# Long convolution with a gated projection on one Trainium2 core: first-stage loads of 16 spread rows, filter products of 128 rows by 200 columns, twiddles on GpSimd

## The chip, the core and the metric

The kernel runs on one core of a Trainium2 chip. A core has five engines that run their own instruction queues: TensorE (PE, matrix products into PSUM; its weight loads are shown apart as PEld), VectorE (DVE), ScalarE (ACT), GpSimd (POOL) and SyncE (SP, which here only issues transfers). Transfers between the device memory (DRAM) and the on-chip memory (SBUF, 128 partitions) run on 16 DMA engines; SP, ACT and POOL each issue transfers on queues of their own. The metric is the device time of one execution in microseconds (us), as a median of several runs.

## The reference

Inputs `x` and `v` are (4, 12800, 128). A small network makes a filter as long as the sequence; `u = x * v` is convolved with it along the sequence, gated by `x`, and then goes through a short causal convolution, a sigmoid gate and two projections.

```python
h_filt = (np.maximum(pos_emb @ w1, 0.0) @ w2) * np.exp(-0.01 * np.arange(S))[:, None]
y = irfft(rfft(x * v, 2 * S, axis=1) * rfft(h_filt, 2 * S, axis=0), 2 * S, axis=1)[:, :S]
x2 = x * y
gate = sigmoid(sum(conv_w[k] * shift(x2, KC - 1 - k) for k in range(KC)))
out = (gate * (x2 @ w_val)) @ w_out
```

## The kernel before

The sequence index is split as S = 12800 = J x N1 x N2 with J = 2 halves, N1 = 100 and N2 = 64. The long transform becomes one over n1 (100 values, index k1 after it), a twiddle, and one over n2 (64 values, k2 after it). Three stages follow each other:

1. First stage (pools `p1`, `ps1`; lines 237 to 394): the transform over n1 of `u`, written to the DRAM tensor `a_u`, and beside it the whole transform of the filter, which stays on the chip in `ag`.
2. Second stage (lines 397 to 527): for 50 pairs of k1, load `a_u`, transform over n2, multiply by the filter's spectrum, transform back, write to `c_y`.
3. Third stage (line 536 on): transform back over n1, multiply by `x`, short convolution, sigmoid, projections, output.

**First stage, the signal.** The host lays `x` and `v` out for each n2: two groups of two batches (h), each with 50 rows, because row n1 is folded with row 99 - n1 (index l). A group is filled up with 14 zero rows to 64, so that the two groups take partitions 0 to 63 and 64 to 127. One `fetch` (line 309) loads 128 rows of 8 KB into one of five tiles `held`; a sixth tile holds rows of `pos_emb`. The 64 values of n2 are taken in the order `n_seq`: q, 63 - q for q = 0 to 31. `product` (314) multiplies x by v on DVE. `mirrored` (320) makes sum and difference of the two of a pair q (tile `eo`, two buffers), and the difference over l. `spectra(q, s)` (329) multiplies with the table `fold`, 64 rows at a time, into PSUM `fp`, and ACT copies the result to `st`. `store` (343) writes rows 0 to 95 from ACT's queue and rows 96 to 99 from POOL's.

**First stage, the filter.** The generator `filt` (253) is worked off in pieces between the signal's steps: 16 parts of `pos_emb @ w1` (PE line 257, then DVE line 260 into `g_sb`, and the next load of `pos`); then the products over n1, with 4 columns e of the filter per piece (lines 275 and 276: one e, 64 columns wide, cosine and sine into the lower and upper 64 rows of `ap`; ACT copies them into `ag`, line 277); then 25 pieces of twiddles: ACT scales a 128 x 128 table by a column of `tw` (line 286), DVE adds the other scaled table (line 289, `fk`), PE multiplies `ag` by `fk` (line 297), ACT copies back (line 300).

**The order** is written out by hand (`tc.manual_schedule()`), so each engine runs its instructions in the order of the code. The main loop (line 368) has 64 steps n, two (s = 0, 1) for each q. In a step come: the fetch of n + 7, the product of n + 3, in even steps the sums of pair q + 1, the spectra of n, then pieces of the filter, then the store of n. Each piece yields a weight (1.5 for a part, 1.0 and 1.7 for products, 1.9 for twiddles); pieces are taken until their weights reach the share (n + 1) / 58 of the total of 115.2, so the filter is done by step 58. SP's queue has the fetches and the loads of `pos`; POOL's has the small stores, the early tables, and nothing else in this stage.

**Second stage, buffers.** `load_pair` takes tiles from the same pool `ld` (six tiles of 8 KB a partition): one table tile for each four pairs, one data tile a pair.

Of the kernel before, what the change touches and what calls it, by code (L numbers as in the profile page):

```python
# [23 lines left out]
B, S, D, FO, KC = 4, 12800, 128, 64, 5  # L24
J, N1, N2 = 2, 100, 64
M = N1 * N2
KG = 8
NF, NH = N1 // 2, 64
R = 4
WARM = 2  # L30
NC1 = N1 // 2 + 1
EDGE = J * N1 - 128


def _tables():
# [5 lines left out]
    off = 2 * np.pi * (np.outer(2 * n1[:NF] + 1, 4 * k1 + 1) % (8 * N1)) / (8 * N1)  # L41
    fold = np.zeros((128, 3, 128))
    for r in (0, NH):
        fold[r:r + NF, 0, :N1] = np.cos(off) + np.sin(off)
        fold[r:r + NF, 1, :N1] = np.cos(off) - np.sin(off)
    fold[:, 2] = 2 * fold[:, 0].astype(np.float32)


# [81 lines left out]
def tile_longconv_gate(  # L130
# [54 lines left out]
    xr_first = const.tile([D, R * B * N1], F32, name="xr_first")  # L185

    def load():
        return ld.tile([128, 2048], F32, name="ld")

    ag_pool = ctx.enter_context(tc.tile_pool(name="ag", bufs=1))  # L190
    ag = ag_pool.tile([128, N1, J, FO], F32, name="ag")
    ld_pool = tc.tile_pool(name="ld", bufs=6)
    ld = ld_pool.__enter__()


    CR = R * B * D
# [25 lines left out]
    def load_pair(p, n1=None):  # L222
        if p % PG == 0:
            n_p = min(PG, NP - p)
            wt = load().rearrange("p (k c e) -> p k c e", k=PG, c=4)[:, :, 0:3]
            nc.sync.dma_start(out=wt[:, 0:n_p], in_=t_w[:, p:p + n_p])
            weights.append(wt)
        a2 = load().rearrange("p (k j e) -> p k j e", k=2, j=J)
        if n1:
            load_a(a2, p, 0, n1)  # L230
        else:
            nc.sync.dma_start(
                out=a2.rearrange("p k j e -> p k (j e)"),
                in_=a_u[2 * p:2 * p + 2].rearrange("k s n e j b d -> (s n e) k (j b d)"))
        return a2, weights[-1][:, p % PG]

    with tc.tile_pool(name="p1", bufs=1) as p1, tc.tile_pool(name="ps1", bufs=1, space=PSUM) as ps1:
        g_sb = p1.tile([N1, J, FO, N2], F32, name="g_sb")

        GN, E, XB = 8, 4, 5  # L240
        held = [load() for _ in range(XB + 1)]
        PE1 = GN // 2 * N1
        pos_held = held.pop()[:, 0:2048 // PE1 * PE1].rearrange("p (i q a) -> p i q a", q=GN // 2, a=N1)
        parts, pos_ts = [(c0, j) for c0 in range(0, N2, GN) for j in range(J)], []

        def load_pos():
            if len(pos_ts) < len(parts):
                c0, j = parts[len(pos_ts)]
                t = pos_held[:, len(pos_ts) % (2048 // PE1)]
                nc.sync.dma_start(out=t.rearrange("p q a -> p (q a)"), in_=pos[j, c0 // GN])  # L250
                pos_ts.append(t)

        def filt():
            for i, (n0, j) in enumerate(parts):
                gp = ps1.tile([N1, GN, FO], F32, name="gp", bufs=2)
                for q in range(GN // 2):
                    nc.tensor.matmul(
                        out=gp[:, 2 * q:2 * q + 2].rearrange("a n e -> a (n e)"),
                        lhsT=pos_ts[i][:, q], rhs=w1bd, start=True, stop=True)
                nc.vector.scalar_tensor_tensor(  # L260
                    g_sb[:, j, :, n0:n0 + GN], gp.rearrange("a n e -> a e n"), 0.0,
                    win[:, j, n0:n0 + GN].unsqueeze(1).to_broadcast([N1, FO, GN]),
                    op0=ALU.max, op1=ALU.mult)
                load_pos()
                yield 1.5

            for j in range(J):
                for e0 in range(0, FO, E):
                    ap = ps1.tile([128, E, N1], F32, name="ap", bufs=2)
                    for e in range(E):  # L270
                        terms = [(j, 0, 1)] if j == 0 else [(1, 0, 1), (0, 1, 2)]
                        for i, (jj, wr, wi) in enumerate(terms):
                            lhs = g_sb[:, jj, e0 + e]
                            fl = dict(start=(i == 0), stop=(i == len(terms) - 1))
                            nc.tensor.matmul(out=ap[0:N2, e], lhsT=lhs, rhs=fwd[:, wr], **fl)
                            nc.tensor.matmul(out=ap[N2:2 * N2, e], lhsT=lhs, rhs=fwd[:, wi], **fl)
                    nc.scalar.copy(
                        out=ag[:, :, j, e0:e0 + E].rearrange("p k e -> p e k"), in_=ap)
                    yield 1.0 + 0.7 * j

            after = None
            for k0 in range(0, N1, 4):
                fk = p1.tile([128, 4, 2 * N2], F32, name="fk", bufs=2)
                for i in range(4):
                    k1 = k0 + i
                    nc.scalar.activation(fk[:, i], dft[:, 1], AF.Copy, scale=tw[:, 1, k1:k1 + 1])
                for i in range(4):
                    k1 = k0 + i
                    nc.vector.scalar_tensor_tensor(
                        fk[:, i], dft[:, 0], tw[:, 0, k1:k1 + 1], fk[:, i], op0=ALU.mult, op1=ALU.add)  # L290
                if after:
                    after()

                def after(k0=k0, fk=fk):
                    gz = ps1.tile([128, 4, 2 * N2], F32, name="gp", bufs=2)
                    for i in range(4):
                        nc.tensor.matmul(
                            out=gz[:, i], lhsT=ag[:, k0 + i].rearrange("p j e -> p (j e)"), rhs=fk[:, i],
                            start=True, stop=True)
                    nc.scalar.copy(out=ag[:, k0:k0 + 4].rearrange("p k j e -> p k (j e)"), in_=gz)  # L300
                yield 1.9
            after()
            yield 0.5

        XE = B * D // 2

        n_seq = [n for q in range(N2 // 2) for n in (q, N2 - 1 - q)]

        def fetch(i):
            t = held[i % XB]  # L310
            nc.sync.dma_start(out=t, in_=xv[n_seq[i]].rearrange("h q w j l b d -> (h q) (w j l b d)"))
            fetched[i] = t.rearrange("p (w e) -> p w e", w=2)

        def product(i):
            t = fetched.pop(i)
            u = p1.tile([128, J * 2 * XE], F32, name="u", bufs=1) if i % 2 == 0 else t[:, 0]
            nc.vector.tensor_tensor(u, t[:, 0], t[:, 1], op=ALU.mult)
            us[i] = u

        def mirrored(q):  # L320

            a, b = us.pop(2 * q), us.pop(2 * q + 1)
            eo = held_e[q % 2]
            for s, op in ((0, ALU.add), (1, ALU.subtract)):
                nc.vector.tensor_tensor(eo[:, s].rearrange("p j l e -> p (j l e)"), a, b, op=op)  # L325
                nc.vector.tensor_tensor(eo[:, s, :, 0], eo[:, s, :, 0], eo[:, s, :, 1], op=ALU.subtract)
            eos[q] = eo

# [20 lines left out]
        fetched, us, eos = {}, {}, {}  # L349
        with tc.manual_schedule():  # L350
            held_e = [p1.tile([128, 2, J, 2, XE], F32, name=f"eo{i}") for i in range(2)]
            fetch(0)
            raws = [
                (dst, _raw(p1, tables, src, f"raw{i}"))
                for i, (dst, src) in enumerate(((wval, w_val), (wout, w_out), (cw, conv_w.rearrange("k d -> d k"))))]
            fil = filt()
            narrow = (None for dst, raw in raws for _ in _narrow(nc, p1, dst, raw))
            n_fil, spent = 16 * 1.5 + 16 * 1.0 + 16 * 1.7 + 25 * 1.9 + 0.5, 0.0
            for i in range(1, XB):
                fetch(i)  # L360
                load_pos()
            product(0)
            product(1)
            mirrored(0)
            product(2)
            for i in (XB, XB + 1):
                fetch(i)
            for n in range(N2):
                q, s = divmod(n, 2)
                if n + XB + 2 < N2:  # L370
                    fetch(n + XB + 2)
                if n + 3 < N2:
                    product(n + 3)
                if s == 0 and q + 1 < N2 // 2:
                    mirrored(q + 1)
                st = spectra(q, s)
                while spent < n_fil * (n + 1) / (N2 - 6):
                    step = next(fil, None)
# [18 lines left out]
    with tc.tile_pool(name="p2", bufs=1) as p2, tc.tile_pool(name="psz", bufs=1, space=PSUM) as psz, \  # L397
# [62 lines left out]
        with tc.manual_schedule():  # L460
            for p in range(-1, NP + 1):
# [52 lines left out]
                    v_p[p] = va, vc, vd  # L514
                if nxt:
                    spectrum(p + 1, 1)
                if old:
# [259 lines left out]
```

## Time and profile before

| | |
|---|---|
| median of three runs | 1134.86 us (1127.76 to 1135.0) |
| profiled execution | 1130.9 us, of it the profiled span 1128.9 us |
| mean granted TensorE clock | 0.972 |
| busy share of the span | PE 92%, PEld 43%, DVE 87%, ACT 55%, POOL 62% |
| data moved | HBM read 225.76 MB, written 131.07 MB |
| of it by queue, share of the 16 DMA engines' span | SP's 224.74 MB, 55.0%; ACT's 129.18 MB, 29.3%; POOL's 2.94 MB, 0.9% |

The page has one execution, in parts: busy time by engine; the span in 40 slices of 28.2 us with a digit for the busy tenths; the DMA queues; the chain of work that ended last, followed backwards; the costliest groups of instructions, named by line of the kernel, engine, operation, output and inputs; and the transfers. In rows of groups, `x64` is a count; then come busy time and mean ns of one, then the engine's idle time before them and who ended it. In rows of the timeline the first number is the start in us, the second the duration. The store of POOL in step n (line 345) is a handy mark of the step. In the chain, `DMA ld<-in_xv_dram`, the loads of x and v, has 17% of the span; the three largest PE lines of the second stage together have 31%.

### The profile page before, as it was taken

The page shows a single profiled execution, that of the slowest core. Times are in us where ns is not written, and L with a number is a line of the kernel's source. Part 1 is how long each engine was busy: PE and PEld are TensorE (multiplying, and loading weights), DVE is VectorE, ACT ScalarE, POOL GpSimd, SP SyncE. Part 2 cuts the span into 40 slices and gives each one's busy share as a digit, 9 for nine tenths or more (in the row PEclk, how much of TensorE's full clock was granted, in tenths as well). Part 3 has the DMA queues.
Part 4 walks back from the last instruction along what each step waited for, and adds up shares of the span by engine and source line. Part 5 has one row for each costly group of instructions (what it writes and reads, how often), then busy time and mean ns, then how long its engine had stood idle before and what let it go on. Part 6 is the DMA issues. An engine that isn't in the chain of part 4 may idle for free.

```text
span 1128.9 us, 17155 instructions
## 1 busy us (share of the span) xinstructions
PE 1038.0 (92%) x6204; PEld 490.9 (43%) x6204; DVE 980.8 (87%) x1214; ACT 619.1 (55%) x1003; POOL 698.1 (62%) x405
## 2 busy tenths in 40 slices
PE   5789997977868999999999999979999999999996
PEld 2345654534423444444444444434444444444442
DVE  6677657888817999999999999739999999999997
ACT  1347665866642444444344444346767777767673
POOL 1111110100016888898898889638999899999981
PEclk9899999999986999999999999998999999999999
DMA  9999999999987788888988999566888888888842
GB/s 376 414 415 410 395 380 368 391 371 372 338 263 245 257 302 310 304 298 309 315 302 288 373 339 329 163 193 262 342 318 346 305 349 314 350 313 351 314 181 116
DMA packets 87771, 357.95 MB, mean 317 GB/s; under 512 B 9269, under 2 KB 18278, under 8 KB 65073
## 3 DMA queue, kind: packets, MB, share of 16 engines
q1 hardware_dynamic: 45768, 224.74, 55.0%
q10 hardware_dynamic: 39408, 129.18, 29.3%
q0 software_dynamic: 2512, 2.94, 0.9%
q8 instruction: 50, 0.82, 0.3%
q14 instruction: 33, 0.26, 0.1%
HBM read 225.76 MB, written 131.07 MB: 316 GB/s over the span
## 4 chain that ended last, share of the span: by engine, by line
PE 63%; DMA 22%; DVE 11%; ACT 3%; issue 1%; SPq 0%; ACTq 0%; DVEq 0%
PE c_ps L442 20%; DMA ld<-in_xv_dram 17%; PE sd L601 9%; PE z_ps L426 9%; PE o_ps L664 7%; PE v_ps L654 6%; PE tp L615 5%; PE fp L338 3%; DMA ld<-in_pos_dram 3%; PE c_ps L411 2%; DVE gt L643 2%; DVE eo L325 2%; DMA c_y<-c_sb 1%; DVE va L432 1%; DVE vb L432 1%
## 5 line engine op out<-in xcount | busy, mean ns | idle before, releaser
L628 POOL TENSOR_TENSOR ext<-yr,xr 128x400 f32<-128x400 f32 x120 | 304.4, 2538 | 38.1 <-DVE yr L626 32.7
L643 DVE SCALAR_TENSOR_TENSOR gt<-ext,cw,gt 128x1600 f32<-128x1600 f32 x128 | 242.7, 1896 | 2.4 <-ACT gt L640 2.4
L338 PE MATMUL fp<-eo,fold 64*128 64x512 f32 x768 | 194.8, 643 | 35.2 <-ACT st L340 19.0
L446 ACT COPY c_sb<-c_ps 128x1024 f32<-128x1024 f32 x100 | 101.3, 1013 | 207.3 <-PE c_ps L442 207.3
L345 POOL DMA_DIRECT2D a_u<-st x64 | 33.2, 519 | 290.4 <-ACT st L340 245.2
L340 ACT COPY st<-fp 128x1024 f32<-128x1024 f32 x128 | 126.7, 1016 | 117.9 <-PE fp L338 81.7
L442 PE MATMUL c_ps<-va,ld 64*128 64x512 f32 (+1 forms) x800 | 165.7, 554 | 0.0
L432 DVE TENSOR_TENSOR va<-z_ps,h_sb 128x2048 f32<-128x2048 f32 x50 | 114.5, 2290 | 30.4 <-PE z_ps L426 30.4
L426 PE MATMUL z_ps<-ld 64*64 64x512 f32 x800 | 123.0, 619 | 9.8 <-DMA ld<-a_u 8.7
L601 PE MATMUL sd<-ag,fold 100*64 100x512 f32 (+1 forms) x512 | 127.9, 617 | 2.9 <-DMA ag<-c_y 2.9
L509 POOL TENSOR_TENSOR va<-va,vb 128x1024 f32<-128x1024 f32 x49 | 116.0, 2367 | 15.9 <-DVE vb L432 15.9
L338 PEld LDWEIGHTS fp<-eo,fold 64*128 64x128 f32 x768 | 73.4, 199 | 115.4 <-issue 59.8
L442 PEld LDWEIGHTS c_ps<-va,ld 64*128 64x128 f32 x800 | 74.1, 189 | 112.2 <-issue 111.7
L664 PE MATMUL o_ps<-gd,wout 128*128 128x400 f32 x256 | 111.5, 517 | 10.7 <-DVE gd L659 9.8
L513 POOL TENSOR_TENSOR va<-va,vb 128x1024 f32<-128x1024 f32 x50 | 119.1, 2383 | 0.0
L432 DVE TENSOR_TENSOR vb<-z_ps,h_sb 128x2048 f32<-128x2048 f32 x50 | 114.0, 2281 | 0.0
L608 ACT COPY sd_sb<-sd 128x512 f32<-128x512 f32 x128 | 76.7, 599 | 57.6 <-PE sd L601 57.0
L654 PE MATMUL v_ps<-ext,wval 128*128 128x400 f32 x256 | 107.3, 501 | 0.0
L442 PE MATMUL c_ps<-vc,ld 64*128 64x512 f32 x400 | 94.2, 589 | 0.0
L615 PEld LDWEIGHTS tp<-ident,sd_sb 128*128 128x128 f32 x512 | 58.9, 142 | 79.2 <-PE sd L601 48.7
L510 POOL TENSOR_TENSOR vc<-vc,vd 128x768 f32<-128x768 f32 x49 | 89.2, 1820 | 1.9
L615 PE MATMUL tp<-ident,sd_sb 128*128 128x128 f32 x512 | 81.0, 283 | 4.7 <-ACT sd_sb L608 3.4
(86 smaller groups left out, 1484.9 us busy)
## 6 DMA issues: line engine op xcount, KB each, us to landing
ld<-in_xv_dram SPq DMA_DIRECT2D x64, 1024.0 KB
ag<-c_y SPq DMA_DIRECT2D x58, 1024.0 KB
c_y<-c_sb ACTq DMA_DIRECT2D x100, 512.0 KB
a_u<-st ACTq DMA_DIRECT2D x64, 768.0 KB
ld<-a_u SPq DMA_DIRECT2D x48, 1024.0 KB
xr<-in_xt_dram SPq DMA_DIRECT2D x31, 800.0 KB
out_dram<-o_sb ACTq DMA_DIRECT2D x31, 800.0 KB
ld<-in_tab_w_dram SPq DMA_DIRECT2D x12, 768.0 KB
```

The lines of the kernel that those rows point to most:

```text
L338: nc.tensor.matmul(out=fp[:, h], lhsT=fold[r, w], rhs=eo[r, o, :, l], start=i == 0, stop=i == len(terms) - 1)
L340: nc.scalar.copy(out=st[:, o].rearrange("k j (h b) d -> k h j (b d)", h=2), in_=fp)
L426: nc.tensor.matmul(out=zs[c][half[h]], lhsT=wk[half[c], 0, half[h]], rhs=a2[half[c], h, j], start=True, stop=True)
L432: nc.vector.tensor_tensor(out, z.rearrange("p (b d) -> p b d", d=D).unsqueeze(1).to_broadcast([128, n, B, D]), h_sb.unsqueeze(2).to_broadc ...
L442: nc.tensor.matmul(out=c_ps[:, h, 0:n], lhsT=wk[half[h], 1 + c], rhs=vt[half[h]].rearrange("p b d -> p (b d)"), start=(i == 0), stop=(i == ...
L513: nc.gpsimd.tensor_tensor(va[:, 2:4], va[:, 2:4], vb[:, 2:4], op=ALU.add)
L601: nc.tensor.matmul(out=sd[c * N2:(c + 1) * N2], lhsT=inv[k, s // NG, c], rhs=ct[c][k, r * B * D:(r + 1) * B * D], start=True, stop=True)
L615: nc.tensor.transpose(out=tp[:, b], in_=t[:, b], identity=ident)
L628: nc.gpsimd.tensor_tensor(e[:, r0 + r], yr, xr, op=ALU.mult)
L643: nc.vector.scalar_tensor_tensor(gt, rows(t, k), cw[:, k:k + 1], gt, op0=ALU.mult, op1=ALU.add)
L654: nc.tensor.matmul(out=v_ps, lhsT=wval, rhs=rows(t)[:, r * ROW:(r + 1) * ROW], start=True, stop=True)
L664: nc.tensor.matmul(out=o_ps, lhsT=wout, rhs=gd, start=True, stop=True)
```

## The change

The change is in the first stage and in how tiles of `ld` are handed out.

*Loads.* The host now lays out one block for each pair q, with both of its n2 (index e) in a row of 16 KB. The 50 rows of a group are spread over its 64 partitions: 48 of them on the partitions whose number modulo 8 is 0 to 5, two more on 6 and 38 (`QROW`); the table `fold` is spread in the same way. A fetch loads partitions r, r + 8, ..., r + 120 with one transfer, for r = 0 to 5 from SP's queue, and the four rows at 6, 38, 70 and 102 with one from POOL's. Zero rows are no longer loaded, except with q = 0, which has all eight r; the tiles of q = 1 and 2 are cleared once by DVE and POOL. There are three tiles of two slots each in place of five of one.

*The order.* In an odd step come the product of pair q + 2 (two instructions) and the fetch of q + 5, which writes the tile that this product has read; the sums stay in even steps. `pos` is loaded in four transfers into the still empty `ag`.

*The filter.* A product over n1 takes two e as 128 columns of weights and both halves of the table as 200 columns; ACT's copy of one piece falls into four, of 64 partitions and 200 columns each. The scaling of the twiddle tables moves from ACT to POOL. The weights become 0.33, 1.0 and 0.9, with a total of 60.3.

*Second stage.* Slots of `ld` come from a list `spare`; a data slot goes back after its pair's second `spectrum`, a table slot after the last use of its four pairs.

```diff
+KX = 6
+QROW = np.array([8 * (q // 6) + q % 6 if q < 48 else 6 + 32 * (q - 48) for q in range(NF)])
...
-        fold[r:r + NF, 0, :N1] = np.cos(off) + np.sin(off)
+        fold[r + QROW, 0, :N1] = np.cos(off) + np.sin(off)
...
     def load():
-        return ld.tile([128, 2048], F32, name="ld")
+        return ld[:, spare.pop(0)]
...
+    ld = ld_pool.__enter__().tile([128, 6, 2048], F32, name="ld")
+    spare, used = [4, 5, 0, 1, 2, 3], {}
...
+        def load_pos(i):
+            nc.sync.dma_start(out=pos_ts[:, 4 * i:4 * i + 4].rearrange("p i q a -> p (i q a)"), in_=pos[i])
...
-                yield 1.5
+                yield 0.33
...
-                    ap = ps1.tile([128, E, N1], F32, name="ap", bufs=2)
...
+                    ap = ps1.tile([128, E // 2, 2, N1], F32, name="ap", bufs=2)
+                    for e in range(E // 2):
+                        terms = [(j, 0)] if j == 0 else [(1, 0), (0, 1)]
+                        for i, (jj, w) in enumerate(terms):
+                            nc.tensor.matmul(
+                                out=ap[:, e].rearrange("p c k -> p (c k)"),
+                                lhsT=g_sb[:, jj, e0 + 2 * e:e0 + 2 * e + 2].rearrange("p e n -> p (e n)"),
+                                rhs=fwd[:, w:w + 2].rearrange("p c k -> p (c k)"),
+                                start=(i == 0), stop=(i == len(terms) - 1))
+                    for h in range(2):
+                        for c in range(2):
+                            nc.scalar.copy(
+                                out=ag[c * N2:(c + 1) * N2, :, j, e0 + h:e0 + E:2].rearrange("p k e -> p e k"),
+                                in_=ap[h * N2:(h + 1) * N2, :, c])
+                    yield 1.0
...
-                    nc.scalar.activation(fk[:, i], dft[:, 1], AF.Copy, scale=tw[:, 1, k1:k1 + 1])
+                    nc.gpsimd.tensor_scalar_mul(fk[:, i], dft[:, 1], tw[:, 1, k1:k1 + 1])
...
-                yield 1.9
+                yield 0.9
...
+        def fetch(q):
+            t = ld[:, 2 * (q % XB):2 * (q % XB) + 2].rearrange("p e n -> p (e n)")
+            for r in range(KX if q else 8):
+                nc.sync.dma_start(out=t[r:128:8], in_=xv[q, r])
+            if q:
+                nc.gpsimd.dma_start(out=t[KX:128:32], in_=xv[q, KX, 0:16:4])
+            fetched[q] = t.rearrange("p (e w n) -> p e w n", e=2, w=2)
+
+        def product(q):
+            t = fetched.pop(q)
+            us[q] = p1.tile([128, 2, J * 2 * XE], F32, name="u", bufs=1)
+            for e in range(2):
+                nc.vector.tensor_tensor(us[q][:, e], t[:, e, 0], t[:, e, 1], op=ALU.mult)
...
+            for q in range(1, XB):
+                (nc.vector, nc.gpsimd)[q - 1].memset(ld[:, 2 * q:2 * q + 2], 0.0)
             fetch(0)
+            load_pos(0)
...
+            product(0)
+            mirrored(0)
+            for q in range(1, XB):
+                fetch(q)
+                load_pos(q)
+            load_pos(XB)
             product(1)
...
                 if s == 0 and q + 1 < N2 // 2:
                     mirrored(q + 1)
+                if s == 1 and q + 2 < N2 // 2:
+                    product(q + 2)
+                    if q + 2 + XB < N2 // 2:
+                        fetch(q + 2 + XB)
                 st = spectra(q, s)
```

More of the change, by code (lines that the diff above doesn't have):

```diff
@@ L43, in _tables @@
     for r in (0, NH):
-        fold[r:r + NF, 0, :N1] = np.cos(off) + np.sin(off)
-        fold[r:r + NF, 1, :N1] = np.cos(off) - np.sin(off)
+        fold[r + QROW, 0, :N1] = np.cos(off) + np.sin(off)
+        fold[r + QROW, 1, :N1] = np.cos(off) - np.sin(off)
     fold[:, 2] = 2 * fold[:, 0].astype(np.float32)
@@ L187, in load @@
     def load():
-        return ld.tile([128, 2048], F32, name="ld")
+        return ld[:, spare.pop(0)]
     ag_pool = ctx.enter_context(tc.tile_pool(name="ag", bufs=1))
     ag = ag_pool.tile([128, N1, J, FO], F32, name="ag")
-    ld_pool = tc.tile_pool(name="ld", bufs=6)
-    ld = ld_pool.__enter__()
+    ld_pool = tc.tile_pool(name="ld", bufs=1)
+    ld = ld_pool.__enter__().tile([128, 6, 2048], F32, name="ld")
+    spare, used = [4, 5, 0, 1, 2, 3], {}
     CR = R * B * D
@@ L224, in load_pair @@
             n_p = min(PG, NP - p)
+            used["w", p // PG] = spare[0]
             wt = load().rearrange("p (k c e) -> p k c e", k=PG, c=4)[:, :, 0:3]
@@ L227, in load_pair @@
             weights.append(wt)
+        used["a", p] = spare[0]
         a2 = load().rearrange("p (k j e) -> p k j e", k=2, j=J)
@@ L238, in tile_longconv_gate @@
         g_sb = p1.tile([N1, J, FO, N2], F32, name="g_sb")
-        GN, E, XB = 8, 4, 5
-        held = [load() for _ in range(XB + 1)]
+        GN, E, XB = 8, 4, 3
         PE1 = GN // 2 * N1
[L243 to L251, printed above, removed]
+        parts = [(c0, j) for c0 in range(0, N2, GN) for j in range(J)]
+        pos_ts = ag.rearrange("p k j e -> p (k j e)")[:, 0:len(parts) * PE1].rearrange(
+            "p (i q a) -> p i q a", q=GN // 2, a=N1)
+        def load_pos(i):
+            nc.sync.dma_start(out=pos_ts[:, 4 * i:4 * i + 4].rearrange("p i q a -> p (i q a)"), in_=pos[i])
         def filt():
@@ L258, in filt @@
                         out=gp[:, 2 * q:2 * q + 2].rearrange("a n e -> a (n e)"),
-                        lhsT=pos_ts[i][:, q], rhs=w1bd, start=True, stop=True)
+                        lhsT=pos_ts[:, i, q], rhs=w1bd, start=True, stop=True)
                 nc.vector.scalar_tensor_tensor(
@@ L263, in filt @@
                     op0=ALU.max, op1=ALU.mult)
-                load_pos()
-                yield 1.5
+                yield 0.33
             for j in range(J):
                 for e0 in range(0, FO, E):
-                    ap = ps1.tile([128, E, N1], F32, name="ap", bufs=2)
[L270 to L279, printed above, removed]
+                    ap = ps1.tile([128, E // 2, 2, N1], F32, name="ap", bufs=2)
[13 more added lines that the diff above has]
+                    yield 1.0
             after = None
@@ L305, in tile_longconv_gate @@
         XE = B * D // 2
[L307 to L318, printed above, removed]
+        def fetch(q):
[10 more added lines that the diff above has]
+                nc.vector.tensor_tensor(us[q][:, e], t[:, e, 0], t[:, e, 1], op=ALU.mult)
         def mirrored(q):
-            a, b = us.pop(2 * q), us.pop(2 * q + 1)
+            u = us.pop(q)
             eo = held_e[q % 2]
             for s, op in ((0, ALU.add), (1, ALU.subtract)):
-                nc.vector.tensor_tensor(eo[:, s].rearrange("p j l e -> p (j l e)"), a, b, op=op)
+                nc.vector.tensor_tensor(eo[:, s].rearrange("p j l e -> p (j l e)"), u[:, 0], u[:, 1], op=op)
                 nc.vector.tensor_tensor(eo[:, s, :, 0], eo[:, s, :, 0], eo[:, s, :, 1], op=ALU.subtract)
@@ L357, in tile_longconv_gate @@
             narrow = (None for dst, raw in raws for _ in _narrow(nc, p1, dst, raw))
[L358 to L361, printed above, removed]
+            n_fil, spent = 16 * 0.33 + 32 * 1.0 + 25 * 0.9 + 0.5, 0.0
             product(0)
+            mirrored(0)
[3 more added lines that the diff above has]
+            load_pos(XB)
             product(1)
[L364 to L367, printed above, removed]
+            fetch(XB)
+            fetch(XB + 1)
             for n in range(N2):
                 q, s = divmod(n, 2)
[L370 to L373, printed above, removed]
                 if s == 0 and q + 1 < N2 // 2:
                     mirrored(q + 1)
+                if s == 1 and q + 2 < N2 // 2:
+                    product(q + 2)
+                    if q + 2 + XB < N2 // 2:
+                        fetch(q + 2 + XB)
                 st = spectra(q, s)
@@ L516, in tile_longconv_gate @@
                     spectrum(p + 1, 1)
+                    spare.append(used.pop(("a", p + 1)))
                 if old:
@@ L525, in tile_longconv_gate @@
                     inverse(p - 1, 1, ((0, oa[:, 2]), (1, oa[:, 3, 0:PB]), (0, oc[:, 0]), (1, oc[:, 1])))
+                    if p % PG == 0:
+                        spare.append(used.pop(("w", p // PG - 1)))
     ld_pool.__exit__(None, None, None)
@@ L756 @@
     xv = np.stack(pairs, 3)
-    xv = np.concatenate([xv, np.zeros_like(xv[:, :, :NH - NF])], 2)
+    xz = np.zeros(xv.shape[:2] + (NH,) + xv.shape[3:], xv.dtype)
+    xz[:, :, QROW] = xv
+    xz = np.stack([xz[:N2 // 2], xz[:N2 // 2 - 1:-1]], 1).reshape(N2 // 2, 2, 16, 8, -1)
+    xv = np.transpose(xz, (0, 3, 2, 1, 4)).reshape(N2 // 2, 8, 16, -1)
     pos = np.asarray(inputs["pos_emb"]).reshape(J, N1, N2 // KG, KG // 2, 2, FO)
-    pos = np.transpose(pos, (0, 2, 4, 5, 3, 1)).reshape(J, N2 // KG, 2 * FO, KG // 2 * N1)
+    pos = np.transpose(pos, (2, 0, 4, 5, 3, 1)).reshape(4, 4, 2 * FO, KG // 2 * N1)
+    pos = np.transpose(pos, (0, 2, 1, 3)).reshape(4, 2 * FO, 2 * KG * N1)
     feeds[:0] = [("xv", xv), ("xt", xt), ("pos", pos)]
```

## The prediction

> **What bounds the kernel now.** I read the page's slices first, then the table of windows, then the DMA queues. In the slices the first stage is the first eleven or twelve of 40.
>
> ```profile
> PE   5789997977868999999999999979999999999996
> DVE  6677657888817999999999999739999999999997
> DMA  9999999999987788888988999566888888888842
> ```
>
> Windows (length, then busy us of PE, PEld, DVE, ACT, POOL, then granted clock, DMA share, GB/s) of the n1 products, of the twiddles, and of the second stage:
>
> ```profile
> 113.00:141.00 28.00, 28.00 (x318) 17.07 (x318) 19.24 (x27) 19.22 (x21) 3.12 (x6) 1.00 1.01 396
> 226.00:254.00 28.00, 20.77 (x100) 11.19 (x98) 22.82 (x41) 17.60 (x35) 2.60 (x5) 0.94 0.99 370
> 400.00:700.00 300.00, 300.00 (x2204) 132.60 (x2204) 296.28 (x278) 124.38 (x196) 269.63 (x159) 1.00 0.90 314
> ```
>
> The second stage is PE's, 300 of 300 us. In the first the DMA engines are full (0.99 to 1.01), but others stand close behind: PE 28 of 28 in the n1 products, DVE 22.8 of 28 in the twiddles.
>
> Next, the DMA queues over 14 to 310 us (q1 carries SP's loads, q10 ACT's stores, q0 POOL's: packets, MB, share of 16 engines), what the products of line 317 waited for (us, times), and four of the 64 small stores of POOL, one for each step n. The first shown is the 6th (n = 5), the last the 64th (n = 63).
>
> ```profile
> q1 hardware_dynamic: 11192, 66.82, 58.7%
> q10 hardware_dynamic: 6384, 44.83, 37.9%
> q0 software_dynamic: 2210, 2.65, 2.9%
>   DMA ld<-in_xv_dram: 47.6, 19
> 49.15 0.52 POOL L345 DMA_DIRECT2D a_u<-st  x1 [8.93 <-ACT st L340]
> ...
> 141.58 0.52 POOL L345 DMA_DIRECT2D a_u<-st  x1 [3.72 <-ACT st L340]
> 145.94 0.52 POOL L345 DMA_DIRECT2D a_u<-st  x1 [3.84 <-ACT st L340]
> ...
> 331.56 0.52 POOL L345 DMA_DIRECT2D a_u<-st  x1 [2.58 <-ACT st L340]
> ```
>
> From n = 5 to n = 63 are 58 steps in 282.4 us, 4.87 each; by the shares loads take 2.86 of it, stores 1.85, the rest 0.15. Where the loads had been fetched ahead a step took 4.36 (141.58 to 145.94). DVE waits 47.6 us for loads in all: more than that no load can give back.
>
> **The change part by part.** *Fewer bytes.* Loads fall from 64 x 1024 KB = 67.1 MB to 2048 + 31 x 1600 KB = 52.9 MB. q1 moves 66.82 / (0.587 x 296) = 0.385 MB per us of all 16 engines, so 14.2 MB less are 37 us. At that rate loads take 2.86 x 52.9/67.1 = 2.25 us a step and DMA 4.25.
>
> *Fewer partitions per load.* One load of 1024 KB over 128 partitions becomes loads of 256 KB into 16 partitions (and 64 KB into 4). The second stage's end has narrow loads of `ag`: 512 KB into partitions 0 to 63, 128 KB into 16 neighbours. First their issue rows; then q1 in 606:608.5 (the first wide one, alone) and in 728:732 (16 neighbours only); then q1 and q10 in 727.5:729.5.
>
> ```profile
> ag<-c_y SPq DMA_DIRECT2D x4, 512.0 KB
> ag<-c_y SPq DMA_DIRECT2D x10, 128.0 KB
> q1 hardware_dynamic: 53, 0.43, 76.6%
> q1 hardware_dynamic: 114, 0.48, 89.0%
> q1 hardware_dynamic: 65, 0.33, 93.4%
> q10 hardware_dynamic: 125, 0.22, 31.0%
> ```
>
> Per us of 16 engines that is 0.43 / (0.766 x 2.5) = 0.225 MB into 64 partitions, 1.71 times slower than 0.385, and 0.48 / (0.89 x 4) = 0.135 MB into 16 neighbours, 2.85 times slower. Which partitions a load writes sets its price. Every eighth partition of 128 has no row here. The ends are 1.0 (spread as wide as a full load) and 2.85 (as few rows as the narrow one); nearest is 1.71, wide but not full. Two things soften it. A load is held up by other loads only, and these hold 0.587 of the time: 1 + 0.71 x 0.587 = 1.42, so loads 3.19 and DMA 5.2 a step. And a store runs beside a load that is held: in the last two rows the queues add up to 124%. I give back a tenth: **4.7 a step**. The ends are 4.25 and, at 1.71 with no softening, 5.85 (2.85 would make 8.4 by the same sum; the range leaves this out). So most of the 37 us are spent again.
>
> [...]
>
> *Issues.* Instead of one issue a step, SP has three and POOL half a one; a POOL issue is 0.52 (rows above) and POOL is busy 2.6 of 28 us, so the cost is cover only, but the order matters (next part). The loads into tiles 1 and 2 wait for a memset of 4096 columns; fetch 0 and the first filter rows, 2.9 MB or 7.5 us of DMA, go first and cover it. The larger filter loads and the earlier filter rows fall into the first five steps, where DMA is full either way; I leave n = 5 at 49 us.
>
> *The n1 products.* Columns here: busy us, mean ns of one, idle before.
>
> ```profile
> L275 PE MATMUL ap<-fwd,g_sb 100*64 100x100 f32 x384 | 37.5, 252 | 0.0
> L297 PE MATMUL gp<-fk,ag 128*128 128x128 f32 x200 | 32.1, 307 | 16.4 <-DVE fk L289 16.4
> L277 ACT COPY ag<-ap 128x400 f32<-128x400 f32 x32 | 26.4, 885 | 7.9 <-PE ap L276 7.9
> L340 ACT COPY st<-fp 128x1024 f32<-128x1024 f32 x128 | 126.7, 1016 | 117.9 <-PE fp L338 81.7
> ```
>
> 384 pairs of 100 columns (line 275 beside line 276) keep PE 37.5 us, 0.98 ns a column; 192 instructions of 200 columns are the same 38,400 columns, and at line 297's 32.1 / (200 x 128) = 1.25 ns a column 48 us at most. PE gains nothing; a step of 4.36 stays one. On ACT one copy of 885 ns becomes four of 200 columns each: 0.44 to 0.885, I take 0.5. The products cost 1.0 each of a budget of 60.3 over 58 steps, 1.04 a step: ACT 126.7/64 + 4 x 0.5 x 1.04 = 4.1 a step (end 5.7). Both lie under 4.7.
>
> *Twiddles on GpSimd.* In that part DVE works in this order (start, us):
>
> ```profile
> 235.50 1.23 DVE L317 TENSOR_TENSOR ld<-ld 128x1024 f32<-128x1024 f32 x1 [2.91 <-DMA ld<-in_xv_dram]
> ...
> 236.82 1.23 DVE L325 TENSOR_TENSOR eo<-u,ld 128x1024 f32<-128x1024 f32 x1
> ...
> 240.56 1.13 DVE L289 SCALAR_TENSOR_TENSOR fk<-dft,tw,fk 128x128 f32<-128x128 f32 x4
> ...
> 241.61 1.22 DVE L317 TENSOR_TENSOR u<-ld 128x1024 f32<-128x1024 f32 x1
> ```
>
> Two steps hold two products of 1.26, 3.74 of sums (236.82 to 240.56), and fk groups of 1.1, now 2 x 1.04/0.9 = 2.31 of them: 8.8 us, 4.4 a step. All these read two SBUF operands. What POOL does beside such an operation the third stage shows: durations (min/median/max ns), then one meeting.
>
> ```profile
> L628 POOL TENSOR_TENSOR ext<-yr,xr x120: 1026/2610/2645, 754.3 to 1102.4; 128x400 f32<-128x400 f32 x120
> L643 DVE SCALAR_TENSOR_TENSOR gt<-ext,cw,gt x128: 1868/1886/2119, 757.5 to 1116.2; 128x1600 f32<-128x1600 f32 x128
> 900.80 1.87 DVE L643 SCALAR_TENSOR_TENSOR gt<-ext,cw,gt 128x1600 f32<-128x1600 f32 x1
> 900.96 2.61 POOL L628 TENSOR_TENSOR ext<-yr,xr 128x400 f32<-128x400 f32 x1 [0.21 <-DVE yr L626]
> L510 POOL TENSOR_TENSOR vc<-vc,vd 128x768 f32<-128x768 f32 x49 | 89.2, 1820 | 1.9
> ```
>
> Alone POOL needs 1.03 us; beside gt 2.61, ending 0.9 after gt ends. POOL stood still while DVE read two operands; DVE lost at most 2119 - 1886 = 233 ns. [...]
>
> By L510 and L628 (1.82 at 768 columns, 1.03 at 400: 2.1 ns a column) a multiply of 128 columns is 0.45 us at most, and half of it at least, with one operand less. It costs DVE 0 to 0.23 when it slips between two sums, all of its 0.45 when DVE's fk waits for it. I take 0.15: 2.31 x 4 x 0.15 = 1.4 per pair of steps. In odd steps POOL first waits, for its load's issue, until the product before the fk group is done: behind it queue that step's multiplies, so DVE waits for an issue (0.52) and one multiply, 0.8. DVE: 8.8 + 1.4 + 0.8 = 11.0, **5.5 a step**; ends 4.4 and (8.8 + 4.2 + 1.0)/2 = 7.0. That is past DMA's 4.7: DVE bounds this part. ACT is relieved, at nothing won.
>
> *Second and third stage.* The slots of `ld` are handed out by a list; there are six as before, two for tables, and PE's 300 of 300 covers a load that comes a step later. Nothing.
>
> **The sum.** Products: 32 x 1.0/1.04 = 31 steps; twiddles 23/1.04 = 22; then 5 steps. 31 x 4.7 + 22 x 5.5 + 5 x 4.7 = 290.2 us against 282.4: plus 7.8. The profiled execution took 1130.9 us (span 1128.9), so 1138.7, say 1139. The runs' median, 1134.86, lies 4 above that execution.
>
> **The rivals.** *Spread rows cost as full ones* (faster): factor 1.0, DMA 4.25; POOL's multiplies slip into DVE's waits. Then PE's 4.36, DVE's 4.5 and 4.25: 31 x 4.36 + 22 x 4.5 + 5 x 4.25 = 255.4, minus 27: 1104; with half of each price 1120. For it: the rows do lie over all 128 partitions. Against: the 64-partition row.
> *Loads stay slow and stores do not fill in* (slower): place, the step's DMA time in products and tail. It decides from 4.9 a step, where the sum passes plus 15. At 5.2: 31 x 5.2 + 22 x 5.5 + 5 x 5.2 = 308, plus 26: 1157; at 5.85 throughout 339, plus 57: 1188. For it: 1.71. Against: the 124%.
> *DVE and POOL take turns in full* (slower): twiddles at 6.5 to 7.0, plus 30 to 41: 1161 to 1172. Against: DVE gave up at most 233 ns to a longer POOL operation.
>
> **How the numbers follow.** My forecast 0.36 (own range 1123 to 1150), full-rate loads 0.34, slow loads 0.18, turns 0.12. The range 1104 to 1172 leaves out the lower end of the first rival (about 0.08) and the upper end of the second (about 0.1). A measurement of this kernel can tell about 1%, here 1123 to 1146 about the runs' median: faster 0.36 (the first rival and a little of mine), same 0.31, slower 0.33 (the two others and the top of mine).
>
> **What would show it.** Right: q1 moves about 0.27 MB per us of 16 engines in the first stage; DMA share stays near 1.0 in the products; POOL multiplies of over 0.5 us and DVE idle with POOL's fk as releaser in the twiddles, steps of 5.5; n = 5 near 49. Wrong: q1 still at 0.38 (first rival), q1 under 0.25 with DVE waiting over 50 us for xv (second), twiddle steps over 6.3 (third), or ACT the one that others wait for in the products, which none of my cases has as the bound.

## The result and the profile after

The changed kernel takes 1179.18 us (median of four runs, 1176.95 to 1185.13), the kernel before 1132.88 beside it: a ratio of 1.0448, 95% interval [1.0413, 1.0484]. It is slower. The profiled execution, the longest of the four, took 1185.13 us with a span of 1183.3, which is 54.4 more than the 1128.9 of before. Here and below the ratios leave out slow executions, among them one of 2069.45 us with the scaling on ACT and one of 1300.51 us with 16 neighbours.

First the slices of the page after: PE, DVE, the DMA engines' share, and what these moved.

```profile
PE   2588887988879599999999999978999999999996
DVE  3584766488887589999999999946999999999997
DMA  9999999999989668888888999866888888888842
GB/s 211 248 324 317 315 317 289 305 313 271 266 269 308 230 241 296 303 305 308 300 307 311 320 358 329 271 168 232 310 326 344 321 328 329 325 347 317 343 186 112
```

The DMA row is as full as before, and yet PE and DVE start at 2 and 3 tenths: the engines that move data are busy and move little. The table of windows says how little, after (columns as in the prediction) and then before in the start:

```profile
14.00:28.00 14.00, 6.88 (x28) 3.64 (x28) 6.10 (x6) 2.03 (x2) 0.55 (x1) 1.00 1.01 206
113.00:141.00 28.00, 20.91 (x86) 9.66 (x84) 17.34 (x26) 20.16 (x32) 4.43 (x8) 0.94 0.97 315
```

```profile
14.00:28.00 14.00, 13.87 (x66) 7.15 (x62) 12.43 (x15) 4.05 (x4) 1.63 (x3) 1.00 1.01 410
```

206 GB/s in place of 410 at the same share of 1.01, and PE 6.9 us of 14 in place of 13.9. In 113:141 it is 315 for 396, and PE, 28 of 28 before, when more products fell into this window, stands idle for a quarter.

Where the 54 us lie, the stores that mark the steps show. Steps n = 36 and 58 before (5 and 63 stand in the prediction), then n = 5, 36, 58 and 63 after:

```profile
199.32 0.52 POOL L345 DMA_DIRECT2D a_u<-st  x1 [3.40 <-ACT fk L286]
...
314.00 0.52 POOL L345 DMA_DIRECT2D a_u<-st  x1 [9.65 <-ACT st L340]
```

```profile
76.74 0.52 POOL L353 DMA_DIRECT2D a_u<-st  x1
...
244.21 0.56 POOL L353 DMA_DIRECT2D a_u<-st  x1
...
371.29 0.52 POOL L353 DMA_DIRECT2D a_u<-st  x1 [3.40 <-ACT st L348]
...
385.85 0.52 POOL L353 DMA_DIRECT2D a_u<-st  x1 [2.58 <-ACT st L348]
```

| stretch | before | after | difference |
|---|---|---|---|
| to n = 5 (start) | 49.15 | 76.74 | +27.6 |
| n = 5 to 36 (31 steps; after, the products; before, also the last parts and the first twiddles) | 4.84 a step | 5.40 | +17.3 |
| n = 36 to 58 (22 steps, twiddles) | 5.21 a step | 5.78 | +12.4 |
| n = 58 to 63 | 3.51 a step | 2.91 | -3.0 |

They add up to 54.3: the second and third stage are as they were, as the prediction had it.

At the start the loads hold up ACT more than DVE. What ACT's copies `st` waited for the loads of x and v (us, times, longest of one), after, then the same before (us, times):

```profile
ACT st L348 <- DMA ld<-in_xv_dram: 52.0, 9, 26.9
```

```profile
  DMA ld<-in_xv_dram: 23.9, 6
```

The copies do not read x and v; the stores between them wait. In both traces the transfers of SP and ACT carry eight completion semaphores in turn, and of those in the first 320 us (146 before, 230 after) none is issued before the last one with its semaphore has landed. After, a pair has six transfers from SP where it had two. So the store of step 0, whose copy ended at 24.7 us, was issued at 51.25, when the load of pair 3 with its semaphore had landed (51.17), and ACT's next copy came behind it, at 51.63. The chain of work that ended last runs through these two (start and duration, us):

```profile
37.11 14.06 DMA ld<-in_xv_dram
...
51.25 9.61 DMA a_u<-st
```

The queues in 113:200, mostly products, before, then after; with after come the loads of the start and of the whole stage (14:28 first, 14:340 last):

```profile
q1 hardware_dynamic: 2575, 18.79, 56.9%
q10 hardware_dynamic: 1960, 13.71, 39.7%
```

```profile
q1 hardware_dynamic: 392, 2.77, 95.9%
...
q1 hardware_dynamic: 1534, 12.57, 49.4%
q10 hardware_dynamic: 1885, 13.21, 43.2%
q0 software_dynamic: 781, 1.03, 4.2%
...
q1 hardware_dynamic: 6176, 49.30, 55.6%
```

As rates of 16 engines: loads 18.79 / (0.569 x 87) = 0.380 MB/us before, 12.57 / (0.494 x 87) = 0.292 after, and 2.77 / (0.959 x 14) = 0.206 at the start, where no store of ACT runs beside them. Of those 2.77 MB, 1.1 are the filter's rows, which go to all 128 partitions; beside the spread rows (0.213) they moved no faster (0.201, by packet size; 0.381 in the same window before, in rows of 1600 bytes for 6400). The stores fell too, from 0.397 to 0.351. Share times step gives what a step costs the DMA engines: loads 2.75 us before and 2.67 after, for a fifth fewer bytes; stores 1.92 and 2.33; POOL's queue 0.10 and 0.23.

In the twiddles, a meeting of POOL and DVE after (the timelines of the two engines):

```profile
296.27 2.34 POOL L293 TENSOR_SCALAR fk<-dft,tw 128x128 f32<-128x128 f32 x4
...
299.16 4.87 POOL L293 TENSOR_SCALAR fk<-dft,tw 128x128 f32<-128x128 f32 x4
...
307.02 0.61 POOL L319 DMA_DIRECT2D ld<-in_xv_dram  x1 [2.48 <-DVE u L326]
307.67 4.65 POOL L293 TENSOR_SCALAR fk<-dft,tw 128x128 f32<-128x128 f32 x8
```

```profile
298.90 1.39 DVE L333 TENSOR_TENSOR eo<-u 128x1024 f32<-128x1024 f32 x1
...
304.37 2.36 DVE L326 TENSOR_TENSOR u<-ld 128x1024 f32<-128x1024 f32 x2
308.31 4.07 DVE L296 SCALAR_TENSOR_TENSOR fk<-dft,tw,fk 128x128 f32<-128x128 f32 x7 [1.58 <-POOL fk L293]
```

Four multiplies take 2.34 us where DVE waits for them and 4.87 beside DVE's sums. At 304.37 the product starts; POOL's load issue waits 2.48 us for it, the multiplies queue behind the issue, and DVE then waits 1.58 for the first.

### The profile page after: what moved, and what is told of

Same layout as the page of the kernel before. It is cut to its first block, busy times and chain, and to the rows that moved or that the text cites. A ratio compares the mean times of both kernels' runs of the same rounds, so it can differ in the third digit from the quotient of the medians.

```text
span 1183.3 us, 16364 instructions
## 1 busy us (share of the span) xinstructions
PE 1058.2 (89%) x5628; PEld 493.4 (42%) x5628; DVE 1001.2 (85%) x1215; ACT 628.6 (53%) x999; POOL 807.9 (68%) x537
## 4 chain that ended last, share of the span: by engine, by line
PE 49%; DVE 21%; DMA 19%; ACT 4%; SPq 3%; issue 2%; POOL 2%; ACTq 0%; DVEq 0%
PE c_ps L453 11%; DMA ld<-in_xv_dram 10%; PE sd L615 10%; DMA a_u<-st 8%; PE o_ps L678 7%; PE v_ps L668 6%; PE tp L629 5%; PE z_ps L437 5%; DVE va L443 5%; DVE vb L443 5%; SPq L317 3%; PE fp L346 3%; DVE u L326 3%; DVE vc L443 2%; DVE vd L443 2%
## 5 line engine op out<-in xcount | busy, mean ns | idle before, releaser
L346 PE MATMUL fp<-eo,fold 64*128 64x512 f32 x768 | 204.9, 672 | 55.6 <-ACT st L348 36.7
L346 PEld LDWEIGHTS fp<-eo,fold 64*128 64x128 f32 x768 | 76.6, 209 | 145.2 <-issue 69.1
L333 DVE TENSOR_TENSOR eo<-u 128x1024 f32<-128x1024 f32 x64 | 79.2, 1238 | 57.3 <-PE fp L346 56.9
```

What stands on the lines that cost most here:

```text
L346: nc.tensor.matmul(out=fp[:, h], lhsT=fold[r, w], rhs=eo[r, o, :, l], start=i == 0, stop=i == len(terms) - 1)
```

## The experiments

Two things were to be told apart: whether the spread rows (placement) cost the time or the new order, and whether the twiddles on GpSimd cost anything of their own. Each ratio is to runs of the kernel before on the same chip; "after" in the lists of edits is the changed kernel. Steps are marked by POOL's stores, as above. Where rows take other partitions, `fold` and the host's layout follow; the diffs leave this out.

**Whole loads in the new order.** One transfer of 128 partitions a pair, zero rows and all; order, products and twiddles as after.

```diff
-            for r in range(KX if q else 8):
-                nc.sync.dma_start(out=t[r:128:8], in_=xv[q, r])
-            if q:
-                nc.gpsimd.dma_start(out=t[KX:128:32], in_=xv[q, KX, 0:16:4])
+            nc.sync.dma_start(out=t, in_=xv[q].rearrange("r i n -> (r i) n"))
```

> The changed kernel, but each pair q is loaded by one transfer of 2048 KB over all 128 partitions, zero rows included; nothing else differs. Theory (placement: the 16 spread rows of a load get in each other's way): loads return to 0.38 MB per us of 16 engines, the step n = 5 from 77 to about 50 us, steps of the products from 5.40 to 4.9, twiddle steps about 5.6, in all 1136 (1126 to 1146), although 28% more bytes are loaded than by the changed kernel. Rival (order: a whole pair must land before its product, three tiles of two slots, the filter rows in four large loads): the placement does not matter, n = 5 stays at 72 to 77 and the time at 1172 to 1186, or above it for the extra bytes.

1135.34 us, ratio 1.0065 [1.004, 1.0091]. Steps n = 5, 36 and 58:

```profile
53.16 0.52 POOL L350 DMA_DIRECT2D a_u<-st  x1 [5.08 <-ACT st L345]
...
206.16 0.55 POOL L350 DMA_DIRECT2D a_u<-st  x1 [1.28 <-ACT st L345]
...
320.32 0.52 POOL L350 DMA_DIRECT2D a_u<-st  x1 [3.40 <-ACT st L345]
```

With more bytes than after it is 44 us faster: products 4.94, twiddles 5.19. The new order and work account for 4 us of the start (53.16 for 49.15), the loads for 23.6: their placement and their number together, for here one transfer replaces seven.

**Whole loads for the first three pairs only.**

```diff
+            if q < XB:
+                nc.sync.dma_start(out=t, in_=xv[q].rearrange("r i n -> (r i) n"))
+            else:
 ...
```

> The changed kernel, but the first three pairs are loaded over 128 partitions by one transfer each; from the fourth on the loads are 16 spread rows as in the change. Placement theory: the late start is the price of loads alone on the queues; n = 5 falls from 77 to 50 to 54 us, steps after it stay at 5.3, in all 1155 (1148 to 1162). Order rival: the start is late because pairs and filter rows are waited for in large lumps; n = 5 stays at 70 to 77 and the time at 1172 to 1186.

1164.28 us, ratio 1.0322 [1.0293, 1.0351], 2 us outside the first range; n = 5 at 62.95, where 50 to 54 was expected. The size missed: pair 3 is spread again, and 20 us lie between steps 0 and 1 here too (POOL's stores at 19.37 and 39.36; after, 31.19 and 53.84). Products (5.23) and twiddles (5.75) stay near after's, as placement says.

**96 neighbouring partitions.** The 50 rows of one group end where those of the other begin; one transfer of partitions 16 to 111 and two of two rows.

```diff
+                nc.sync.dma_start(out=t[16:112], in_=x[16:112])
+                for p in (14, 112):
+                    nc.gpsimd.dma_start(out=t[p:p + 2], in_=x[p:p + 2])
```

> The changed kernel with the valid rows as 100 neighbours (partitions 14 to 113, the table spread to match): one transfer of 96 neighbouring partitions and two of 2 per pair, the same bytes as the change. [...] Rival (any load of fewer than 128 partitions is slow, as both narrow loads of the kernel before were): loads at 0.2 to 0.27 and a time of 1170 to 1200. Order rival: 1172 to 1186.

**Six loads of 16 neighbours**, bytes and number of transfers as after.

```diff
+                for p in (0, 16, 32, 64, 80, 96):
+                    nc.sync.dma_start(out=t[p:p + 16], in_=x[p:p + 16])
+                for p in (48, 112):
+                    nc.gpsimd.dma_start(out=t[p:p + 2], in_=x[p:p + 2])
```

> The changed kernel with rows 0 to 47 of each group on partitions 0 to 47 and 64 to 111: six loads of 256 KB into 16 neighbouring partitions each, and two of 2 rows from POOL; the same bytes, number and size of loads as the change. Placement theory: loads alone at 0.13 to 0.15 MB per us of 16 engines, as the 16 neighbours of the kernel before; DMA about 7 a step, in all 1280 (1230 to 1340). Rival (the number and size of the transfers make them slow, not the rows they write): 1170 to 1190, as the change.

The first took 1192.37 us, ratio 1.0561 [1.0537, 1.0586], as the rival of slow loads has it; the second 1279.85, as expected. q1 in 14:40, 96 neighbours, then 16:

```profile
q1 hardware_dynamic: 661, 5.90, 88.4%
```

```profile
q1 hardware_dynamic: 586, 4.00, 93.0%
```

0.257 and 0.165 MB/us (after: 0.224 in the same window). For transfers of the same number and size, 16 neighbours cost 101 us more than 16 spread rows, so the rows' place counts. But 96 neighbours are slow as well: n = 5 comes 7 us earlier than after, at 69.81, but later steps lose that again, which was not taken apart. What makes them slow no run here shows.

**32 rows at every 4th partition**, in place of 16 at every 8th; bytes and order as after.

```diff
-            for r in range(KX if q else 8):
-                nc.sync.dma_start(out=t[r:128:8], in_=xv[q, r])
+            for r in range(3 if q else 4):
+                nc.sync.dma_start(out=t[r:128:4], in_=x[r])
-                nc.gpsimd.dma_start(out=t[KX:128:32], in_=xv[q, KX, 0:16:4])
+                nc.gpsimd.dma_start(out=t[3:128:32], in_=x[3, 0:32:8])
```

> The changed kernel, bytes and order kept, but with 32 rows at a time at every 4th partition (three transfers of 512 KB for a pair, the four rows left over from GpSimd) in place of 16 at every 8th. [...] If any load of fewer than 128 rows is slow, as the 96 neighbours were, it comes near the changed kernel: 1165 (1150 to 1185).

1139.04 us, ratio 1.0076 [1.005, 1.0102]: 40 us less than after, and 11 under the lower end for slow loads. (The transfers are also fewer and larger than after; the next pair of runs keeps their number.) Steps n = 5, 36 and 58, and the queues in 113:200:

```profile
58.24 0.52 POOL L354 DMA_DIRECT2D a_u<-st  x1 [0.23 <-issue]
...
199.41 0.56 POOL L354 DMA_DIRECT2D a_u<-st  x1
...
325.17 0.52 POOL L354 DMA_DIRECT2D a_u<-st  x1 [3.40 <-ACT st L349]
```

```profile
q1 hardware_dynamic: 1365, 14.86, 46.5%
q10 hardware_dynamic: 2121, 14.91, 45.6%
```

q1 is back at 14.86 / (0.465 x 87) = 0.367 MB/us, the stores at 0.376, and the products run at 4.55 a step, 0.29 under before. The start (58.24; 49.15 before) and the twiddles (5.72; 5.21 before) stayed slower. With the loads out of the way the twiddles kept after's pace, so something else sets them.

**32 rows at every 4th partition against neighbours, all from SP.** Two kernels with four transfers a pair each: 32, 32, 32 and 4 spread rows, or 32, 32, 18 and 18 neighbours. The first edit is to the kernel of every 4th partition.

```diff
-                nc.gpsimd.dma_start(out=t[3:128:32], in_=x[3, 0:32:8])
+                nc.sync.dma_start(out=t[3:128:32], in_=x[3, 0:32:8])
```

> As the run with every 4th partition, but the four rows left over are issued by SP in place of GpSimd. Theory: the twiddles' 5.72 a step there came from GpSimd's load issue, which waits for DVE's product (14.7 us of GpSimd idle in 230:310) with the next multiplies queued behind it; without it the twiddle steps fall to 5.0 to 5.2, as in the run with whole loads, and the time from 1139 to 1126 (1119 to 1132). Rival: GpSimd's multiplies and DVE slow each other whatever the queue; the steps stay at 5.7 and the time at 1139 (1134 to 1143).

```diff
+                for p, z in ((0, 32), (64, 32), (32, 18), (96, 18)):
+                    nc.sync.dma_start(out=t[p:p + z], in_=x[p:p + z])
```

> As the every-4th-partition kernel with all loads from SP, the same bytes in the same four transfers a pair, but in neighbouring partitions: 32, 32, 18 and 18 of them. [...]

The first took 1132.34 us, ratio 1.0021 [0.9996, 1.0046], just over the upper end expected; the second 1190.22 us, ratio 1.0527 [1.0476, 1.0578]. Loads in 14:28, spread rows, then neighbours:

```profile
q1 hardware_dynamic: 697, 5.29, 101.2%
```

```profile
q1 hardware_dynamic: 346, 2.73, 99.7%
```

0.373 against 0.196 MB/us, at a full share in both, with one order, equal bytes and as many transfers: 58 us by the partitions (pair 0 comes as one whole load in the second, which if anything helps it). n = 5 comes at 54.78 and 81.00, a step of products takes 4.78 and 5.73 us. The number of transfers counts for less: seven a pair from SP at every 8th partition (a run below) took 1183.47 us, these four neighbours 1190.22.

**The scaling back on ACT, loads as after.**

```diff
-                    nc.gpsimd.tensor_scalar_mul(fk[:, i], dft[:, 1], tw[:, 1, k1:k1 + 1])
+                    nc.scalar.activation(fk[:, i], dft[:, 1], AF.Copy, scale=tw[:, 1, k1:k1 + 1])
```

> The changed kernel with the scaling of the twiddle tables back on ACT; the loads stay spread. If the slow loads set the twiddles' steps (placement), these stay at 5.5 to 5.8 us and the time is 1174 (1167 to 1181). If GpSimd's multiplies and their turns with DVE set them, the steps fall to about 5.2 and the time is 1166 (1160 to 1170), 0.55 x 22 = 12 us less.

1164.58 us, ratio 1.0299 [1.023, 1.0369], 15 us less than after. Steps n = 36, 58 and 63 (of an execution of 1172.34 us):

```profile
244.50 0.52 POOL L353 DMA_DIRECT2D a_u<-st  x1 [5.17 <-ACT st L348]
...
355.68 0.52 POOL L353 DMA_DIRECT2D a_u<-st  x1 [3.03 <-ACT st L348]
...
376.14 0.52 POOL L353 DMA_DIRECT2D a_u<-st  x1 [2.58 <-ACT st L348]
```

n = 36 is where it was; the twiddles fall from 5.78 to 5.05 a step. So the slow loads alone do not set this part; GpSimd does. (Of the 15.6 us that n = 58 comes earlier, the last five steps give 5.9 back, so the stage ends 9.7 earlier.)

**Only the scaling on GpSimd, else as before; and only the new products, else as before.** Their edits are those two parts of the change.

> The kernel before with only the scaling of the twiddle tables moved to GpSimd. Placement theory: with full-rate loads the move costs little, as in the run with whole loads, whose twiddle steps were 5.19 with GpSimd's multiplies: 1131 (1127 to 1136). Theory of turns between DVE and GpSimd: the twiddle steps grow by the 0.57 seen in the changed kernel, 1142 (1138 to 1150).

> The kernel before with only the new n1 products, 128 rows by 200 columns, and their four ACT copies. Placement theory: these steps are the DMA engines' at 4.84 and stay so, 1130 (1126 to 1135). Rival, that four copies in place of one hold the products' steps (4.84 to 5.40 in the changed kernel): 1146 (1140 to 1152).

1125.57 us, ratio 0.9967 [0.9942, 0.9993], a little under what was expected, and 1133.68, ratio 1.0035 [1.0007, 1.0064], as expected. Windows of the first in the twiddles and of the second in the products:

```profile
226.00:254.00 28.00, 23.08 (x108) 11.88 (x107) 25.96 (x39) 14.80 (x17) 27.84 (x29) 0.94 1.00 388
```

```profile
113.00:141.00 28.00, 24.15 (x110) 13.09 (x109) 18.80 (x32) 27.46 (x47) 2.65 (x5) 1.00 0.96 337
```

Alone, the move to GpSimd costs nothing and may win 0.3%: POOL becomes full (27.84 of 28), but beside DMA engines that were full already, with 100 multiplies in 24 steps and no load in its queue. The same move cost 15 us in the changed kernel, where they fall into 22 steps and stand behind POOL's loads: the price of a part depends on what else sets its step. The products cost 4 us by the medians, and ACT is their bound, 27.5 of 28 us: four copies of 0.5 us a piece, at up to two pieces a step where the changed kernel has 1.04.

**The leftover rows from SP, loads as after.** Is it GpSimd's load issue, with the multiplies queued behind it?

```diff
-                nc.gpsimd.dma_start(out=t[KX:128:32], in_=xv[q, KX, 0:16:4])
+                nc.sync.dma_start(out=t[KX:128:32], in_=xv[q, KX, 0:16:4])
```

> The changed kernel with the four rows left over issued by SP in place of GpSimd, and nothing else; GpSimd keeps the twiddles' multiplies, the loads stay at every 8th partition. Theory of the queue: twiddle steps from 5.78 to about 5.1, as with the scaling on ACT, start and products unchanged; 1165 (1160 to 1171). If the multiplies themselves cost it: 1179 (1174 to 1185).

1183.47 us, ratio 1.0446 [1.0385, 1.0507]: no gain in the time. Steps n = 5, 36 and 58:

```profile
82.59 0.52 POOL L353 DMA_DIRECT2D a_u<-st  x1 [5.08 <-ACT st L348]
...
252.26 0.55 POOL L353 DMA_DIRECT2D a_u<-st  x1 [2.36 <-ACT st L348]
...
370.75 0.52 POOL L353 DMA_DIRECT2D a_u<-st  x1 [4.09 <-ACT st L348]
```

The twiddles did fall, from 5.78 to 5.39 a step or 8.6 us in all, but n = 5 came 5.9 us later than after (82.59 for 76.74) and the products took 5.47 for 5.40. So the queue is part of the twiddles' price, 0.39 of the 0.73 that the scaling on ACT wins; that the start and the products would stay was wrong, and why the start is later stays open. With the faster loads (every 4th partition) the same edit brought 1139.04 to 1132.34 and the twiddles from 5.72 to 5.31, where 5.0 to 5.2 was expected. What remains there are GpSimd's multiplies (window, then the multiplies of that kernel in 205:320):

```profile
226.00:254.00 28.00, 24.87 (x117) 12.84 (x117) 25.00 (x39) 14.30 (x19) 27.84 (x31) 1.00 0.92 311
```

```profile
L293 POOL TENSOR_SCALAR fk<-dft,tw 128x128 f32<-128x128 f32 x92 | 98.4, 1078 | 0.7
```

POOL is busy 27.84 of 28 us while DMA has room (0.92). A hundred multiplies in 22 steps are 4.55 a step, at 1.078 us, with a store's 0.55: 5.45, about the step of 5.31.

**Every 4th partition and the scaling on ACT.**

> As the run with every 4th partition, with the scaling of the twiddle tables back on ACT and the leftover rows still from GpSimd. With loads near full rate and nothing behind GpSimd's load issue the twiddle steps should be those of the fewer bytes or of DVE, 4.6 to 5.0: 22 x 0.9 = 20 less than 1139, 1119 (1112 to 1127). If the steps stay above 5.5, something other than GpSimd sets them: 1135 or more.

1113.22 us (1111.8 to 1116.28), ratio 0.9846 [0.9807, 0.9885]: 1.5% under the kernel before. Steps n = 5, 36, 58 and 63:

```profile
57.73 0.52 POOL L354 DMA_DIRECT2D a_u<-st  x1 [0.24 <-ACT st L349]
...
195.26 0.52 POOL L354 DMA_DIRECT2D a_u<-st  x1 [2.57 <-ACT fk L293]
...
300.31 0.52 POOL L354 DMA_DIRECT2D a_u<-st  x1 [3.40 <-ACT st L349]
...
315.18 0.52 POOL L354 DMA_DIRECT2D a_u<-st  x1 [2.58 <-ACT st L349]
```

Products 4.44 and twiddles 4.78 a step: the smaller loads do pay (n = 63 at 315 for 332) once their rows lie at every 4th partition and the multiplies are off GpSimd.

## Why the prediction was wrong

It said 1139 (1104 to 1172), with slower at 0.33; the time is 7 over the upper end. Of 46.5 us missed in the profiled executions (54.3 for 7.8), the start has 27.6, the products 21.8 (31 steps of 5.40 for 4.7), the twiddles 6.1, and the last steps give back 8.9.

*"I leave n = 5 at 49 us"* is the largest failure. The argument was that DMA is full there either way. It is (1.01 in 14:28), but the loads moved 0.206 MB/us at that share. The prediction had a rate for narrow rows (0.225 into 64 partitions) and used it for every step but these, in which loads run alone and nothing softens it. The whole-load run gives 23.6 of the 27.6 to the loads. An estimate from the rates: SP's loads of the pairs 0 to 3 are 2.10 + 3 x 1.57 = 6.8 MB, 33 us at 0.206 and 18 at 0.385, so 15 of it; the filter's four loads in the same queue, 3.3 MB, would be 7 more. And the prediction left out a way by which the loads hold the steps: the store of step 0 waited for a load of pair 3, and ACT stood 26.9 us.

*"A tenth given back", 4.7 a step* failed in the products. The softened 5.2 was near the 5.40 measured, but by luck: loads took 2.67 a step for the 3.19 expected and stores 2.33 for 1.85, so part of the price fell on the stores, which the prediction had left at their rate. What was to bring the 5.2 down, a store that runs beside a load that is held, did not show: the queues' shares add up to 97%, and the stores themselves slowed, from 1.92 to 2.33 us a step. The 124% came from a window of 2 us at the end of the second stage; this stage does not repeat it. The second rival, slow loads and stores that do not fill in, was the mechanism. Its sign, q1 under 0.25 MB/us with DVE waiting over 50 us for xv, was wrongly chosen: q1's mean was 49.30 / (0.556 x 326) = 0.272, as the forecast said, and DVE's wait for xv was 16.3 us, for most of the waiting was ACT's, 52.0 us (the first of these groups of 14:340 after is DVE's; the other two are the copies and the matmuls of the products):

```profile
L326 DVE TENSOR_TENSOR u<-ld 128x1024 f32<-128x1024 f32 x56 | 66.0, 1220 | 17.2 <-DMA ld<-in_xv_dram 16.3 <-issue 0.3
...
L283 ACT COPY ag<-ap 64x200 f32<-64x200 f32 x128 | 64.4, 503 | 3.6 <-PE ap L276 2.4
L276 PE MATMUL ap<-fwd,g_sb 100*128 100x200 f32 x192 | 40.6, 349 | 0.0
```

*The price of the placement.* The pattern had no row, and 1.71 was taken from 64 partitions. With no store of ACT beside it the factor is 0.385 / 0.206 = 1.87. Which partitions the rows write decides it here: in 14:28, 32 neighbours came to 0.196 and 32 rows at every 4th partition to 0.373; 16 neighbours, in 14:40, came to 0.165, the filter's rows among it. Why one pattern is slower than another no run shows. The sum without softening, 1188, was the upper end of a rival held at 0.18.

*Products.* "PE gains nothing" held: 40.6 us for the 37.5 of before. The copies, taken at 0.5 us, are 0.503, 64.4 us in all for 26.4. ACT is the bound only in the run with the new products alone, which packs them closer.

*Twiddles, 5.5 a step against 5.78.* Both effects showed again: POOL is slower while DVE reads two operands (four multiplies 4.87 us beside DVE's sums, 2.34 with DVE waiting), and DVE waits for what queues behind POOL's issue (1.58 us in the meeting above). The price of that queue, 0.8 for two steps, was right as well: without POOL's load issue a step is 0.39 shorter with the slow loads and 0.41 with the faster ones. A multiply takes 0.59 us with DVE waiting, not 0.45 at most, and DVE's `fk` operations take 456 ns (median) beside POOL's multiplies, for 347 before, with the scaling on ACT. And the prediction asked only what POOL costs DVE; where the loads are fast POOL itself is full, 27.84 of 28. The runs with ACT give the size of it, 15 us on the slow loads and 26 on the faster ones (1139.04 to 1113.22). Turns in full, the third rival, did not come: its sign was a step over 6.3.

*Issues* were put at cover only. Their busy time stayed small (POOL's 28 load issues take 16.8 of the 326 us of 14:340); the waits that came with more transfers, above, were left out. *Later stages* cost nothing, as forecast; the last five steps, put at 4.7, took 2.91; the last load of x and v had been issued by 349 us, 22 before n = 58.

The first rival, full-rate loads at 1104 to 1120, came true in time with every 4th partition, though only with the scaling on ACT.

## What to carry to other kernels

In these runs a load's time went by the partitions that its rows wrote, and not only by bytes: before cutting zero rows from a load, see that the rows that are left still lie in a pattern that moves near the full rate, here every 4th partition (0.373 MB/us of 16 engines; 0.385 for whole loads) and not every 8th (0.206). A full DMA share says nothing about the rate: at a share of 1.01 the engines moved 410 GB/s before and 206 after. Where loads run alone, as at the start, the slower rate was not hidden (23.6 of the 27.6 us lost there were the loads'), and not paid only by the engine that reads the data: here ACT waited longest (26.9 us), since its stores were issued behind the loads. An engine that seems free (POOL at 2.6 of 28 us) is priced by what works beside it: here a multiply took 1.08 us in the mean with POOL full, and 0.59 where DVE waited for it.

## What was not expected of the hardware

With one load of 96 neighbouring partitions (16 to 111) a pair q1 moved 0.257 MB/us in 14:40, with 32 rows at every 4th partition 0.371, though the first writes three times as many partitions at once; no run here shows why, and it stays open. What ran beside the slow loads was slow as well: stores, which read other tiles, moved 0.351 MB/us in 113:200 for 0.397 before, and the filter's rows 0.201 in 14:28 for 0.381. And four multiplies on GpSimd took 2.34 us with DVE waiting and 4.87 beside DVE's sums, while DVE's sums gave up little (1.39 for 1.23 us) and its shorter `fk` operations nearly a third (456 for 347 ns).
